# The opening of a fused attention and feed-forward kernel, laid out anew up to its first product with w_out

## The chip, the cores and the metric

The kernel runs on one core of one Trainium2 chip. A core has five engines with a queue of instructions each: TensorE (PE in the profile), VectorE (DVE), ScalarE (ACT), GpSimd (POOL) and SyncE (SP). Each engine works through its own queue in order; between engines semaphores keep the order of data. Loads and stores are issued from SP, ACT and POOL and carried by 16 DMA engines. The metric is the device time of one execution in microseconds; less is better.

## The reference

Two layers follow each other. The first is linear attention with decay over 64-row blocks, for 4 batches, 8 heads, 768 rows and 64 columns a head:

```python
for b in range(nb):
    intra = einsum('bhic,bhjc->bhij', qb, kb) * Dmask[None]
    intra = einsum('bhij,bhjd->bhid', intra, vb)
    inter = einsum('bhid,bhde->bhie', qb * lam_pow[None], kv_state)
    out[:, :, sl] = intra + inter
    kb_dec = kb * rev_pow[None]
    kv_state = lam_block[None, :, None, None] * kv_state + einsum('bhsd,bhse->bhde', kb_dec, vb)
```

`Dmask`, `lam_pow`, `rev_pow` and `lam_block` are powers of a decay `lam`, one per head. The second layer takes the result as 3072 tokens of 512 columns:

```python
h = x @ w_in                                   # 512 x 2048
g = maximum(h, 0) + alpha * minimum(h, 0)      # alpha per column of w_in
return g @ w_out                               # 2048 x 512
```

Inputs and output are 32-bit floats; the products run in 16-bit floats.

## The kernel before, in words

**Tiling.** The attention uses blocks of 128 rows, two at a time (256 rows, even and odd rows apart). Tokens go in six chunks `c` of 512: 256 rows of two batches (`bi` 0 and 1). A *unit* is one chunk, one batch and one half of the heads (`hh`): `units[n]`, so chunk 0 holds units 0 to 3 (units 0 and 1 are batch 0, units 2 and 3 batch 1), chunk 1 units 4 to 7. Of the two blocks of chunk 0 the first has no state before it.

**Steps of a unit.** `load` (L85 to L92, from SP, 32-bit) and `load16` (L102, from POOL, cast to 16 bits on the way) bring keys, queries and values; a whole load covers both halves of the heads, and with a part it covers one. `hold` (L85) writes one element of the tile of a later key load from DVE; that load, in SP's queue, can be issued only after it. `cast` makes 16-bit keys (`"k"`) or queries (`"q"`) on the engine that the call names (A is ACT, V is DVE, G is POOL). `turn` transposes keys and queries on PE into the bank `tp` (tag `tk`), and `turned` copies them to `qkT`. `key_decayed` multiplies keys by their decay (`kdec`), `decayed` does so with the queries (`qdT`). `cluster(old, new)` is the unit pair's work on PE: for `old` its queries times the state before (L389, from `RD`) and the masked scores times values (L409), for `new` its scores (L365) and keys times values (L426). With `True` its result goes into the banks b0 and b1 that the second layer uses as well, otherwise into `acc`. `masked` is DVE's product of scores and decay mask (L438). `state` keeps or updates the state (`KV` on ACT at L473 and L476, `R` on DVE), `spread` writes it into `RD`, and `out_of` copies the attention's result into `xT`.

**The second layer.** `up(c, f, bi, slot)` multiplies 128 columns of w_in by `xT` into bank b0, b1 or b2 (`slot`): 512 wide for `bi` None, 256 wide for one batch (four products each, L511). `below` takes the negative part on ACT (L522), `gate` combines both on DVE with `oma`, which is 1 - alpha (L534); only after that is the bank free. `down` multiplies by w_out (L544), `store` writes out. `load_win(i)` and `load_wout(i)` bring a quarter of the weights each, from POOL. w_in's first quarter serves columns `f` 0 to 3.

**Decays.** lam is loaded from ACT's queue first of all. `logs` takes its logarithm (DVE L198, ACT L199), `logs_by_pair` lays it out by pairs of heads (L203, L204), `mask_logs(hh)` makes four mask logarithms on DVE (L217) and `mask_exp(hh)` their Exp on ACT (L228); `key_decay`, `state_decay` and `query_decay` are Exp on ACT too. `zeros` fills the eight `RD` tiles with zeros on DVE (L177). `positions` and `distances` make the row distances (POOL, then DVE, `pos_f` last at L195). `identity` makes the matrix that transposes need, on POOL. `slopes` turns alpha on PE and makes `oma`.

**Fills.** `fill(n, slot)` issues n matmuls of 128x128 of a constant tile into a bank, whose result nobody reads (L257).

**What sets the order.** The kernel is written with its order by hand: each call in the list emits its instructions at once on the queues of its engines, in the order of the list, and no scheduler moves them. Buffers come from pools with few copies (five raw key tiles, one tile of scores per half pair, one `tp`), so a step also waits until the former user of its buffer is done. The list runs from `light()` into the third chunk; then a woven loop takes over.

## Time and profile before

| What | Value |
|---|---|
| median of 3 runs | 217.8 us (217.76 to 218.54) |
| the profiled execution | 217.74 us |
| its span | 216.0 us |
| PE busy | 208.6 us (97%), 2224 matmuls |
| DVE, ACT, POOL busy | 136.9, 113.3, 88.9 us |
| granted clock of PE, mean | 1.00 |
| fills before the first w_in product | 163 |
| first w_in product starts | 19.69 us |
| first w_out product starts | 42.27 us |

The profile's busy shares are sums over stages of different kinds: PE's first 8.88 us are fills alone. A row of the timeline gives start, length, engine, line, operation, and in brackets the idle time before it with what ended it. Consecutive instructions of an engine overlap by a little, so the start of the next row, not the end of the length, tells how long an instruction keeps its engine. The time of a load runs from its issue until its data is there.

### The profile page before, as it was taken

What the parts mean: (1) busy time and instruction counts of PE and PEld (TensorE: products, weight loads), DVE (VectorE), ACT (ScalarE), POOL (GpSimd) and SP (SyncE); (2) the same over time, 40 slices, a digit from 0 to 9 for tenths busy, and PEclk for the clock granted to TensorE, in tenths of its full rate; (3) what the DMA queues carried; (4) which work ended last, traced back from release to release, by engine and by line L of the source; (5) the groups of instructions that cost most, each with busy time, mean ns of one, the idle gap of its engine ahead of it and who ended that gap; (6) DMA issues with size and microseconds to landing.
All of it is one profiled execution on the core that took longest, in us unless ns stands there. A gap on an engine that the chain in (4) does not pass through costs nothing.

```text
span 216.0 us, 5454 instructions
## 1 busy us (share of the span) xinstructions
PE 208.6 (97%) x2224; PEld 114.7 (53%) x2224; DVE 136.9 (63%) x280; ACT 113.3 (52%) x222; POOL 88.9 (41%) x146
## 2 busy tenths in 40 slices
PE   8979899989999999999999999999999999999994
PEld 8958555544544555546554554554545444444442
DVE  3976999868597878888976646645746344435000
ACT  3777778841657645548745545545435534444120
POOL 8759547760088890193557266256221000000000
PEclk9999999999999999999999999999999999999999
DMA  5999999999999999987999242193011011110212
GB/s 131 218 195 223 203 210 251 214 167 190 314 273 154 253 157 195 180 178 191 196 279 177 40 100 72 25 100 84 16 49 49 5 49 49 49 43 8 97 49 99
DMA packets 63288, 29.85 MB, mean 138 GB/s; under 512 B 34192, under 2 KB 61088, under 8 KB 63264
## 3 DMA queue, kind: packets, MB, share of 16 engines
q1 hardware_dynamic: 38400, 15.01, 35.0%
q0 software_dynamic: 20368, 8.26, 31.9%
q10 hardware_dynamic: 4496, 6.24, 9.1%
q8 instruction: 17, 0.28, 0.6%
q14 instruction: 7, 0.06, 0.1%
HBM read 27.28 MB, written 6.29 MB: 155 GB/s over the span
## 4 chain that ended last, share of the span: by engine, by line
PE 89%; DVE 4%; ACT 3%; DMA 2%; issue 1%; DVEq 0%; ACTq 0%
PE h_ps L511 38%; PE o_ps L544 32%; PE o_ps L569 6%; PE s L365 4%; PE acc L409 3%; PE acc L389 2%; DMA lam_sb<-in_lam_dram 2%; PE acc L426 1%; DVE dmask L217 1%; DVE RD L177 1%; ACT m L522 1%; DVE g L534 1%; PE op_fill L257 1%; PE tp L318 1%; ACT RD L267 1%
## 5 line engine op out<-in xcount | busy, mean ns | idle before, releaser
L534 DVE SCALAR_TENSOR_TENSOR g<-m,oma,h_ps 128x512 f16<-128x512 f32 (+1 forms) x104 | 72.6, 704 | 50.0 <-ACT m L522 49.2
L511 PE MATMUL h_ps<-xT,w_in_sb 128*128 128x512 f16 (+1 forms) x416 | 95.7, 363 | 0.7 <-DVE g L534 0.7
L522 ACT ACTIVATE m<-h_ps 128x512 f32<-128x512 f32 (+1 forms) x104 | 57.9, 564 | 59.3 <-PE h_ps L511 56.9
L544 PE MATMUL o_ps<-w_out_sb,g 128*128 128x512 f16 x320 | 79.4, 379 | 0.7 <-DVE g L534 0.7
L511 PEld LDWEIGHTS <-w_in_sb 128*128 128x128 f16 x416 | 39.4, 98 | 42.3 <-issue 1.6
L544 PEld LDWEIGHTS <-g 128*128 128x128 f16 x320 | 30.5, 98 | 35.8 <-issue 1.0
L271 POOL COPY RD<-R 64x128 f16<-64x128 f16 x46 | 13.4, 290 | 52.0 <-DVE R L481 47.6
L438 DVE TENSOR_TENSOR sm<-s,dmask 128x512 f16<-128x512 f32 x48 | 31.9, 684 | 3.3 <-PE s L365 3.2
L267 ACT ACTIVATE o_sb<-o_ps 128x512 f32<-128x512 f32 (+1 forms) x24 | 14.2, 593 | 23.1 <-PE o_ps L544 12.5
L347 POOL TENSOR_TENSOR qdT<-qkT,qdecay 128x512 f16<-128x512 f16 (+1 forms) x21 | 20.5, 976 | 9.3 <-ACT qkT L267 4.4
L298 POOL TENSOR_TENSOR kdec<-kraw,kdecay 128x512 f16<-128x512 f32 x19 | 19.9, 1049 | 2.1 <-PE acc L426 1.9
L267 ACT ACTIVATE xT<-acc 128x512 f16<-128x512 f32 x19 | 11.3, 597 | 5.9 <-PE acc L426 4.5
L569 PE MATMUL o_ps<-w_out_sb,g 128*128 128x512 f16 (+2 forms) x80 | 14.0, 336 | 0.0
L257 PE MATMUL op_fill<-spark 128*128 128x128 f16 x163 | 12.5, 243 | 1.2 <-DVE one L183 1.1
L481 DVE SCALAR_TENSOR_TENSOR R<-R,rdecay,acc 128x64 f16<-128x64 f16 x48 | 11.2, 275 | 3.6 <-ACT xT L267 1.9
L257 PEld LDWEIGHTS <-spark 128*128 128x128 f16 x163 | 11.3, 111 | 1.7 <-DVE one L183 1.1
L271 POOL CAST qk<-kraw 128x512 f16<-128x512 f32 x14 | 9.0, 645 | 7.5 <-ACT RD L267 6.7
L102 POOL DMA_DIRECT2D vh<-in_v_dram x13 | 11.7, 904 | 0.0
L569 PEld LDWEIGHTS <-g 128*128 128x128 f16 x80 | 7.2, 98 | 6.9
L365 PE MATMUL s<-qkT 64*64 64x128 f16 x384 | 10.4, 222 | 0.0
L409 PE MATMUL acc<-sm,vh 64*64 64x128 f16 x352 | 9.0, 217 | 0.0
L389 PEld LDWEIGHTS <-RD 128*128 128x128 f16 x80 | 6.3, 98 | 4.8 <-ACT RD L267 0.4
(73 smaller groups left out, 126.3 us busy)
## 6 DMA issues: line engine op xcount, KB each, us to landing
kraw<-in_k_dram SPq DMA_DIRECT2D x10, 512.0 KB, 6.8
out_dram<-o_sb ACTq DMA_DIRECT2D x17, 256.0 KB, 3.0
qraw<-in_q_dram SPq DMA_DIRECT2D x8, 512.0 KB, 7.1
vh<-in_v_dram POOLq DMA_DIRECT2D x11, 256.0 KB, 7.4
w_in_sb<-in_moe_w_in_dram POOLq DMA_DIRECT2D x4, 512.0 KB, 9.5
w_out_sb<-in_moe_w_out_dram POOLq DMA_DIRECT2D x4, 512.0 KB, 8.7
out_dram<-o_sb ACTq DMA_DIRECT2D x12, 128.0 KB, 2.0
kraw<-in_k_dram SPq DMA_DIRECT2D x4, 256.0 KB, 5.3
```

Source lines behind the costliest of these rows:

```text
L257: nc.tensor.matmul(t[:, 0:128], lhsT=spark, rhs=spark, start=True, stop=True)
L267: nc.scalar.activation(out, in_, AF.Copy)
L271: nc.gpsimd.tensor_copy(out=out, in_=in_)
L298: engine(eng).tensor_tensor(out=kdec, in0=kr, in1=d.unsqueeze(3).to_broadcast([128, 2, 4, D]), op=ALU.mult)
L347: engine(eng).tensor_tensor(out=qdT[:, :, :, p], in0=t["qkT"][:, 0, :, :, p], in1=qdecay[:, hh, :, :, p], op=ALU.mult,)
L365: nc.tensor.matmul(s[hl][ds(a * 64, 64), hp, 1 - e, :].rearrange("p (e j) -> p e j", e=2), lhsT=t["qkT"][p, 1, e, hp, ds(a * 64, 64)], rhs ...
L438: nc.vector.tensor_tensor(out=t["sm"][hl], in0=t["s"][hl], in1=mask_of(hl, units[n][2]), op=ALU.mult)
L511: nc.tensor.matmul(h_ps[:, 0:n] if bi is None else h_ps[:, 0:n].rearrange("p (e j) -> p e j", e=2), lhsT=w_in_sb[:, gi, ts(f, 128)], rhs=x ...
L522: nc.scalar.activation(m[:, 0:n], HP[c, f, bi][:, 0:n], AF.Relu, scale=-1.0)
L534: nc.vector.scalar_tensor_tensor(out=g, in0=mv, scalar=oma[:, f : f + 1], in1=hv, op0=ALU.mult, op1=ALU.add)
L544: nc.tensor.matmul(O[c, t], lhsT=G[c, f][:, t // 2, t % 2, :], rhs=w_out_sb[:, f, :], start=(f == 0), stop=(f == NF - 1),)
L569: nc.tensor.matmul(o_ps[:, 0:n], lhsT=G[c, f][:, t // 2, t % 2, :], rhs=w_out_sb[:, f, ds(c0, n)], start=(f == 0), stop=(f == NF - 1),)
```

## The change

Only the hand-written list between `distances()` and the first `gate(0, 15, None)` differs; every function is the same, and so is the list behind it. The same steps are called, apart from fills: 163 fills stand ahead of the first `down` before, 160 after. The calls are in another order, and some are on other engines: the key casts of units 0 and 5 go from POOL to ACT, those of units 3, 4 and 6 from ACT to POOL; `key_decayed` of units 1, 4 and 5 from DVE to POOL, of unit 2 from POOL to DVE; `decayed` of units 2 and 5 from POOL to DVE; `turned` of unit 5 from ACT to DVE, of unit 6 from DVE to ACT; `out_of` of unit 2 from DVE to ACT, of units 3 and 4 from ACT to DVE; `spread` of unit 4 from POOL to ACT, of unit 5 from ACT to POOL. Before the first transposes, in brief:

- `zeros()` stands ahead of `logs()`, behind it before;
- the first queries are loaded ahead of the first keys on SP; POOL's first load is the first values, not queries;
- `hold("k", 0, 1, 0)` stands behind `logs_by_pair()`, and `load("k", 0, 1, 1)` ahead of `load("k", 0, 1, 0)`;
- `load_alpha()` stands ahead of `logs()`.

The diff, cut to the part up to the first products with w_in and the last lines:

```diff
     distances()
+    load16("v", 0, 0, 0)
+    zeros()
+    load("q", 0, 0, 0)
+    fill(12, 2)
     load("k", 0, 0, 0)
+    fill(34, 3)
+    fill(14, 1)
+    fill(6, 3)
+    load_alpha()
     logs()
-    load("q", 0, 0, 0)
-    load16("q", 0, 1)
-    hold("k", 0, 1, 0)
-    fill(40, 0)
-    fill(1, 3)
-    load16("q", 0, 0, 1)
-    zeros()
-    fill(6, 3)
-    fill(38, 0)
-    mask_logs(1)
+    fill(5, 1)
+    identity()
+    cast(0, "k", "A")
     cast(0, "q", "A")
     logs_by_pair()
+    state_decay()
+    hold("k", 0, 1, 0)
+    mask_logs(0)
+    mask_logs(1)
+    load16("q", 0, 0, 1)
+    turn(0)
+    query_decay(0, 1)
     key_decay()
-    identity()
-    load_alpha()
-    fill(14, 2)
+    query_decay(2, 1)
+    turned(0, "V")
+    fill(2, 1)
+    mask_exp(1)
     load("k", 0, 0, 1)
+    cast(1, "k", "V")
+    query_decay(1, 1)
+    slopes(2)
+    load16("v", 0, 0, 1)
+    load16("q", 0, 1)
+    load16("v", 0, 1)
+    fill(18, 1)
+    key_decayed(0, "V")
+    load("k", 0, 1, 1)
+    load_win(0)
+    fill(8, 0)
+    load16("q", 1, 0)
+    decayed(0, "G")
+    fill(10, 1)
     load("k", 0, 1, 0)
-    cast(0, "k", "G")
-    mask_exp(1)
-    turn(0)
-    mask_logs(0)
-    fill(3, 1)
-    fill(12, 1)
-    fill(7, 2)
-    load("k", 0, 1, 1)
-    key_decayed(0, "V")
+    cast(2, "k", "A")
+    turn(1)
+    fill(7, 1)
+    mask_exp(0)
+    cluster(None, 0)
+    load16("v", 1, 0)
+    turned(1, "V")
+    key_decayed(1, "G")
+    hold("k", 2, 1)
+    query_decay(3, 1)
+    key_decayed(2, "V")
+    fill(13, 2)
+    fill(11, 3)
+    state(0, 0)
+    turn(2)
+    masked(0, 1)
+    hold("k", 1, 0)
+    decayed(1, "G")
+    cast(3, "k", "G")
+    load_win(1)
+    masked(0, 0)
+    spread(0, 1, "A", True)
+    cluster(0, 1, True)
+    spread(1, 1, "A", True)
+    key_decayed(3, "G")
+    turned(2, "V")
+    turn(3)
+    masked(1, 1)
+    masked(1, 0)
+    turned(3, "V")
+    cluster(1, None)
+    out_of(0, "A")
+    cluster(None, 2)
     hold("k", 3, 0)
-    load16("v", 0, 0, 0)
...
-    out_of(0, "A")
-    decayed(2, "G")
-    spread(1, 1, "A", True)
-    masked(1, 0)
+    decayed(2, "V")
+    masked(2, 1)
+    out_of(1, "A")
+    up(0, 0, 0, 2)
+    decayed(3, "G")
+    masked(2, 0)
+    load_win(2)
     state(1, 0)
-    cluster(1, None)
-    load_win(2)
...
+    load_win(3)
+    up(0, 1, 0, 1)
     spread(2, 1, "A", True)
...
+    up(0, 2, 0, 0)
+    cluster(2, 3, True)
+    below(0, 0, 0)
     below(0, 1, 0)
...
     up(0, 15, None, 2)
     cluster(None, 6)
+    below(0, 14, None)
     out_of(5, "A")
     up(1, 1, 0, 1)
+    up(1, 2, 0, 0)
+    turn(7)
+    gate(0, 14, None)
     below(0, 15, None)
-    up(1, 2, 0, 0)
-    gate(0, 13, None)
-    gate(0, 14, None)
-    turn(7)
+    fill(7, 2)
+    cast(8, "k", "G")
     down(0, 0, 0, 2)
```

## The prediction

> **What bounds the kernel now.** I read the page's busy table first, then busy time by stretches of the span, then TensorE's waits over the rest of the span, then the chain that ended last, in order of time, and then the timeline and the DMA issues of the opening.

> The page: the span, and TensorE's (PE's) share of it.

> ```profile
> span 216.0 us, 5454 instructions
> PE 208.6 (97%) x2224; PEld 114.7 (53%) x2224; DVE 136.9 (63%) x280; ACT 113.3 (52%) x222; POOL 88.9 (41%) x146
> ```

> Busy time by stretch (start:end, length, then us and instructions of PE, PEld, DVE, ACT, POOL, then granted clock, DMA share, GB/s), cut where PE's work changes.

> ```profile
> 0.00:8.88 8.88, 7.77 (x99) 7.63 (x100) 5.52 (x23) 4.82 (x8) 7.88 (x20) 1.00 0.88 159
> ...
> 19.69:42.27 22.58, 21.79 (x331) 13.52 (x322) 20.90 (x43) 18.00 (x41) 15.05 (x24) 1.00 1.32 219
> 46.23:216.00 169.77, 166.56 (x1513) 83.91 (x1502) 100.70 (x194) 80.74 (x148) 57.22 (x93) 1.00 0.63 121
> ```

> PE's waits from 40 us to the end, the only row of the answer:

> ```profile
> PE o_ps L544 <- DVE g L534: 0.7, 1, 0.7
> ```

> From 46.23 us on PE never waits long enough to be listed, and the list of steps there is unchanged. So a lead or a delay that PE has when the products with w_out begin should come out at the end, one for one. The change is worth what it moves PE at that point. The first 8.88 us hold only fills (matmuls whose result nobody reads), so PE's busy share says nothing there. From 19.69 to 42.27 PE and DVE are both nearly full (21.79 and 20.90 of 22.58 us).

> The chain that ended last, its opening part (start, length, what):

> ```profile
> 0.74 3.76 DMA lam_sb<-in_lam_dram
> ...
> 4.74 0.27 DVE RD L177
> ...
> 6.93 1.19 DVE dmask L217 x4
> ...
> 8.60 1.41 DVE dmask L217 x4
> ...
> 12.21 0.38 PE tp L318 x4
> ```

> It is a DVE chain: lam lands at 4.50, eight zero fills stand until 6.93, then the decay logarithms, key work, the first qkT, and only then PE's second transposes at 12.21.

> **The change, part by part.** The durations are in the timeline (start, us, engine, line, operation); for the spacing of two instructions I take the difference of their starts.

> ```profile
> 1.06 7.99 PE L257 MATMUL op_fill<-spark 128*128 128x128 f16 x99 [1.06 <-DVE one L183]
> 2.20 1.84 POOL L102 DMA_DIRECT2D qh<-in_q_dram  x2
> 2.29 0.29 DVE L195 CAST pos_f<-pos_i 128x256 f32<-128x256 int32 x1
> 5.43 2.41 POOL L102 DMA_DIRECT2D vh<-in_v_dram  x3
> 5.68 0.63 ACT L267 ACTIVATE qk<-qraw 128x512 f16<-128x512 f32 x1 [0.74 <-DMA qraw<-in_q_dram]
> 6.33 1.28 ACT L232 ACT_TABLE_LOAD   x1
> 7.62 0.49 ACT L232 ACTIVATE kdecay<-loglam,rev_f 128x8 f32<-128x8 f32 x2
> 9.33 1.61 PE L257 MATMUL op_fill<-spark 128*128 128x128 f16 x22
> 10.04 0.84 ACT L228 ACTIVATE dmask<-dmask 128x768 f32<-128x768 f32 x1 [1.03 <-DVE dmask L217]
> 10.79 1.26 ACT L240 ACTIVATE qdecay<-pos_f,llp 128x128 f32<-128x128 f32 x4
> 13.40 0.69 DVE L438 TENSOR_TENSOR sm<-s,dmask 128x512 f16<-128x512 f32 x1 [1.24 <-PE s L365]
> 16.43 0.66 ACT L267 ACTIVATE xT<-h_acc 128x256 f16<-128x256 f32 x2 [1.00 <-PE h_acc L426]
> 16.98 0.55 ACT L267 ACTIVATE RD<-h_acc 64x128 f16<-64x128 f32 x2
> 17.55 0.45 ACT L476 ACTIVATE KV<-h_acc 128x128 f32<-128x128 f32 x2
> 19.69 1.05 PE L511 MATMUL h_ps<-xT,w_in_sb 128*128 128x256 f16 x8
> 20.45 0.71 ACT L522 ACTIVATE m<-h_ps 128x256 f32<-128x256 f32 x2
> 20.89 0.86 DVE L534 SCALAR_TENSOR_TENSOR g<-m,oma,h_ps 128x256 f16<-128x256 f32 x2
> 24.00 1.02 ACT L267 ACTIVATE qkT<-tp 128x1024 f16<-128x1024 f16 x1
> 25.87 1.89 PE L511 MATMUL h_ps<-xT,w_in_sb 128*128 128x512 f16 x8 [0.52 <-DVE g L534]
> 27.61 2.10 DVE L534 SCALAR_TENSOR_TENSOR g<-m,oma,h_ps 128x512 f16<-128x512 f32 x3 [0.19 <-ACT m L522]
> ```

> The loads of the opening (tile, issuer, KB in the tile, us from issue to landing), in the order of their issue: the first keys, the first queries, keys of the third part, queries, values, w_in, keys of chunk 1.

> ```profile
> kraw<-in_k_dram SPq DMA_DIRECT2D x1, 256.0 KB, 4.1
> qraw<-in_q_dram SPq DMA_DIRECT2D x1, 256.0 KB, 4.4
> kraw<-in_k_dram SPq DMA_DIRECT2D x1, 256.0 KB, 5.9
> qh<-in_q_dram POOLq DMA_DIRECT2D x1, 128.0 KB, 6.5
> vh<-in_v_dram POOLq DMA_DIRECT2D x1, 128.0 KB, 6.8
> w_in_sb<-in_moe_w_in_dram POOLq DMA_DIRECT2D x1, 512.0 KB, 9.4
> kraw<-in_k_dram SPq DMA_DIRECT2D x1, 512.0 KB, 8.2
> ```

> 1. Zero fills ahead of the logarithms. The 8 x 0.27 us now follow pos_f (2.58) and end at 4.76, in DVE's idle time before lam lands at 4.50. They cost 0.25 us there and free 2.19 later. Pair copies follow (0.48, from 8.12 to 8.60), then eight mask logarithms (1.2 to 1.4 for four): done at about 8.3 instead of 10.0.

> 2. First casts. Queries are now issued first on SP and keys second; both have landed at 5.65. The cast of the first keys goes from POOL to ACT, so ACT has two casts of 0.53 to 0.63, and the table load for Exp starts at 6.85 instead of 6.33. ACT is 0.5 us later there. Behind it come four small decays (0.3 each) and one mask Exp (0.75); ACT is through at 10.4.

> 3. The third keys (unit 2's). The one-element write that holds their load back now stands behind the pair copies: SP issues at about 5.7, not 4.7. With the row's 5.9 us they land at 11.6. ACT's cast of them stands ahead of the mask Exp of the first pairs, so ACT waits from 10.4 to 11.6, and that Exp runs 12.15 to 13.0 instead of 10.04 to 10.88. This is the new wait. (Unit 3's keys, which no held-back load stands ahead of on SP any more, are issued at about 2.3 and land before them; nothing waits for those.) Behind it on ACT are one decay, the copy of state 0 and its spread (to 14.1); DVE waits with the first masked product, PE with the first product with a state.

> 4. PE. Fills before the first transposes fall from 99 to 71: 28 fewer at 1.61/22 = 0.073 us, so 9.05 becomes 7.0, when both casts are ready (6.85). The turn of alpha behind them waits for a load that ACT now issues at 2.75; by the SP rows of 4.1 to 5.9 us it lands at 6.9 to 8.7. I take 8.2, near the upper row, because POOL's loads run beside it. Then 36 fills (2.4) reach 10.7. The second transposes need queries which POOL now issues second (about 3.9, after one issue of 0.92 and the identity): with 6.5 us they land at 10.4. So these transposes run at 10.5 to 11.2, before at 12.21. After 7 fills come scores and the state product (to 12.4, values landed long before: issued first, 2.20 + 6.8 = 9.0), and 24 fills (1.6) reach 13.9.

> 5. To the first w_in product. Unit 2's transposes 13.9 to 14.65; masked products (0.69 each, spaced 0.6) 13.0 to 14.4; qkT copy to 15.35; cluster of units 0 and 1 14.65 to 15.5; unit 3's transposes to 16.3; two masked products and the copy to 17.2 on DVE; spread 0.55, xT 0.66 on ACT to 16.75; last product of unit 1 to 16.95; its xT 0.6 to 17.6. w_in's first quarter is issued at 7.2 instead of 7.8 and lands at 7.2 + 9.4 = 16.6. The first product with w_in starts at 17.8; before, at 19.69. The lead is 1.9, partly because the 28 fills that stood here before are gone.

> 6. What takes part of it back. Three products (0.44 each) now stand ahead of cluster 2/3, which writes into the banks of two of them: it waits for ACT's spread (18.0 to 18.55), three negative parts (0.35 spaced) and two gates (0.43): 19.75 instead of 19.1, a new 0.65 us. Then 11 fills (0.7) stand where PE waits for the spread of unit 3 anyway (21.35). Unit 4's keys, held until 13.7 instead of 12.1, land at 13.7 + 8.2 = 21.9; POOL casts them by 22.5, where PE has waited 0.55. ACT's copy of that qkT (1.02) ends at 24.1 and starts unit 4's scores, another 0.25. The first full-width product starts at 25.1. Before it started at 25.87, but the scores and state of unit 4 (0.47) were still to come: the lead is 25.87 + 0.47 - 25.1 = 1.24.

> 7. From there on the same products go through three banks, each with a negative part on ACT (0.6) and a gate on DVE (0.7). Followed queue by queue, PE stands idle at three banks (0.2, 0.35 and 0.25 us), and the two early columns of chunk 1 end at 40.6. The start of unit 7's transposes marks that place:

> ```profile
> 41.82 0.61 PE L318 MATMUL tp<-ident,qk 128*128 128x128 f16 x8
> ...
> 44.03 1.02 PE L544 MATMUL o_ps<-w_out_sb,g 128*128 128x512 f16 x4 [0.74 <-DVE g L534]
> ```

> The 7 new fills ahead of the first product with w_out stand in the 0.74 us that PE waits there for a gate, so they are covered; were that cover gone, they would cost 0.45. The moves of values, w_in and w_out on POOL's queue keep the total bytes before each need and are counted at nothing: the w_out loads come earlier, the second w_in quarter at 14.6 lands by 24 and is needed at 25.1. If it were 1 us later than that, PE would wait.

> **Sum:** 41.8 - 40.6 = 1.2 us off the span. The profiled execution took 217.74 (span 216.0 and 1.74 around it), 0.06 under the median of 217.8. The forecast is 217.8 - 1.2 = 216.6.

> [...]

> **Rivals.** *The lead goes to the gates (less gain).* From 19.69 DVE is 93% busy, and between the first full-width product and the last gate I count 15.8 us for it (17 gates of 0.43 or 0.7, four masked products, four states, three copies or products of 0.3 to 0.7), about as long as PE's. Against it: DVE was as full before. As a check by sums: PE's fills before the columns of chunk 1 fall from 163 to 153, 10 x 0.066 = 0.65 us. If all else that PE waits for is as long as before, the gain is 0.65 and the time 217.1.

> *Slower: unit 2's keys late.* The place is ACT's cast ahead of the mask Exp. Up to a landing at 11.9 the 24 fills cover it; then each us costs one. At 13.1 the gain is gone. Served in order of issue they stand behind four POOL loads and land at about 12.9: gain 0.2, 217.6. At the 8.2 us of the later keys they land at 13.9: 2.0 us late, 218.6. For it speaks that POOL issues five loads before them; against it that 256 KB took 5.9 us beside two such loads.

> *POOL's first loads late.* If zero fills delay POOL's issue until 4.76, the second queries would land at about 12.4 and all behind shift by 1.5 to 1.9, leaving a loss of 0.5: 218.3. Against it: in this trace three POOL issues beside zero fills took 0.8 us each, like others. [...]

> *More gain.* If the first lead of 1.9 stays whole because unit 4's keys land sooner and the banks are free in time: 215.9.

> **How the numbers follow.** Forecast (gain 0.8 to 1.6) 0.42; gates 0.26; unit 2's keys 0.16; POOL 0.06; more gain 0.10. A difference of 0.5%, 1.09 us, is about what a measurement here can tell. Of the forecast's case 0.31 lies beyond it, with more gain's 0.10 and 0.02 of the gates' that is 0.43 faster. Slower by over 0.5% takes a landing near 14.2 or two of these together: 0.14. The rest, 0.43, is the same. The forecast's own range is 216.2 to 217.0; the whole range runs from more gain's 215.8 to 218.4, between the late cases' 218.3 and 218.6, and leaves out under 2 in 10.

> **What would show it.** Right: second transposes near 10.5, an ACT wait of about 1.2 us for unit 2's keys near 10.4, first w_in product near 17.8, full-width product near 25.1, no new PE wait after 46. Wrong: that ACT wait over 2.5 us, PE waiting for queries, or PE waits of over 1.5 us in sum between 25 and 41.

## The result, and the profile after

The changed kernel took 219.14 us in the median of 20 executions (217.28 to 223.9), the kernel before 217.77 (217.53 to 218.54) beside it. The ratio is 1.005, with a 95% interval of 1.0034 to 1.0066: half a per cent slower, where 0.5% faster was forecast. (The ratio leaves out disturbed executions, the medians do not.) Besides its middle, the spread has changed: 6.6 us between lowest and highest, against 1.0.

The profiled execution took 218.54 us. Its page (span; busy us, share and matmuls; the granted clock of TensorE in 40 slices; the queue that brings instructions, with packets, MB and share):

```profile
span 216.6 us, 5445 instructions
...
PE 209.7 (97%) x2221; PEld 115.5 (53%) x2221; DVE 137.1 (63%) x280; ACT 111.8 (52%) x221; POOL 90.3 (42%) x147
...
PEclk9999699999999999999999999999999999999999
...
q8 instruction: 17, 0.28, 0.5%
```

The clock row has a 6 in its fifth slice; before, all 40 slices have a 9. Busy time by stretch, with the same columns as before:

```profile
18.90:21.60 2.70, 0.80 (x30) 0.54 (x32) 2.38 (x5) 1.24 (x5) 0.70 (x2) 1.00 1.35 214
21.60:24.30 2.70, 2.70 (x64) 2.29 (x64) 0.65 (x2) 2.06 (x7) 1.75 (x3) 0.62 1.25 207
24.30:27.00 2.70, 2.70 (x50) 2.10 (x48) 0.65 (x3) 1.69 (x3) 2.41 (x4) 0.75 1.24 207
27.00:42.78 15.78, 15.55 (x183) 8.71 (x181) 14.56 (x29) 11.19 (x23) 8.19 (x12) 1.00 1.31 216
47.05:216.60 169.55, 166.55 (x1511) 83.86 (x1502) 100.76 (x194) 80.75 (x148) 57.55 (x94) 1.00 0.63 122
```

In 18.90 to 21.60 PE works for only 0.80 of 2.70 us; for 5.4 us after that it is busy all the time, at a granted clock of 0.62 and then 0.75. The long run of products with w_out starts at 47.05 (before 46.23), and the rest takes 169.55 (before 169.77). So the whole loss arises ahead of 47, as the prediction's first part said it must; what it missed lies between 19 and 27. PE's timeline there:

```profile
7.02 0.80 PE L318 MATMUL tp<-ident,qk 128*128 128x128 f16 x8
...
10.04 0.39 PE L318 MATMUL tp<-ident,qk 128*128 128x128 f16 x4
...
17.43 1.48 PE L511 MATMUL h_ps<-xT,w_in_sb 128*128 128x256 f16 x12
19.47 0.27 PE L389 MATMUL h_acc<-qdT,RD 128*128 128x128 f16 x2 [0.55 <-DVE g L534]
19.67 0.42 PE L365 MATMUL s<-qkT 64*64 64x128 f16 x16
19.92 0.23 PE L409 MATMUL h_acc<-sm,vh 64*64 64x128 f16 x3
21.50 0.38 PE L409 MATMUL h_acc<-sm,vh 64*64 64x128 f16 x13 [1.35 <-issue]
...
21.93 1.09 PE L257 MATMUL op_fill<-spark 128*128 128x128 f16 x11
...
42.78 0.61 PE L318 MATMUL tp<-ident,qk 128*128 128x128 f16 x8
```

Up to 19.5 PE runs at about the forecast times or ahead of them: first product with w_in at 17.43 (before 19.69), a lead of 2.26 us. Then, after 3 of 16 products of one group, PE stands 1.35 us, and the releaser is "issue": it waited for nothing that the profile shows. The eleven fills behind it take 1.09 us, at a granted clock of 0.66 from 21.93 to 22.93; in the kernel below with unit 4's keys let go later they take 0.79, and twelve of them in the kernel before, at a granted clock of 1.00, take 0.84. At the transposes of unit 7 the lead of 2.26 has become a lag of 0.96 (42.78 against 41.82).

### The profile page after: what moved, and what is told of

It reads as the page before. It is cut to its first block, busy times and chain, and to the rows that moved or that the text cites. A ratio compares the mean times of both kernels' runs of the same rounds, so it can differ in the third digit from the quotient of the medians.

```text
span 216.6 us, 5445 instructions
## 1 busy us (share of the span) xinstructions
PE 209.7 (97%) x2221; PEld 115.5 (53%) x2221; DVE 137.1 (63%) x280; ACT 111.8 (52%) x221; POOL 90.3 (42%) x147
## 4 chain that ended last, share of the span: by engine, by line
PE 94%; DVE 2%; ACT 1%; issue 1%; DVEq 0%
PE h_ps L511 38%; PE o_ps L544 33%; PE o_ps L569 6%; PE op_fill L257 6%; PE s L365 4%; PE acc L409 3%; PE acc L389 2%; PE tp L318 2%; PE acc L426 1%; DVE g L534 1%; DVE sm L438 1%; ACT m L522 1%; PE tp L314 0%; DVE qkT L269 0%; ACT xT L267 0%
## 5 line engine op out<-in xcount | busy, mean ns | idle before, releaser
L534 DVE SCALAR_TENSOR_TENSOR g<-m,oma,h_ps 128x512 f16<-128x512 f32 (+1 forms) x104 | 72.6, 704 | 52.0 <-ACT m L522 51.3
L511 PE MATMUL h_ps<-xT,w_in_sb 128*128 128x512 f16 (+1 forms) x416 | 96.1, 365 | 0.2 <-DVE g L534 0.2
L522 ACT ACTIVATE m<-h_ps 128x512 f32<-128x512 f32 (+1 forms) x104 | 58.2, 564 | 60.3 <-PE h_ps L511 58.5
L544 PE MATMUL o_ps<-w_out_sb,g 128*128 128x512 f16 x320 | 79.4, 379 | 0.1
L511 PEld LDWEIGHTS <-w_in_sb 128*128 128x128 f16 x416 | 39.9, 99 | 42.0 <-issue 1.2
L544 PEld LDWEIGHTS <-g 128*128 128x128 f16 x320 | 30.5, 98 | 35.2 <-issue 0.4
L438 DVE TENSOR_TENSOR sm<-s,dmask 128x512 f16<-128x512 f32 x48 | 31.9, 684 | 0.7 <-PE s L365 0.6
L267 ACT ACTIVATE o_sb<-o_ps 128x512 f32<-128x512 f32 (+1 forms) x24 | 14.2, 593 | 23.1 <-PE o_ps L544 12.5
L298 POOL TENSOR_TENSOR kdec<-kraw,kdecay 128x512 f16<-128x512 f32 x21 | 22.0, 1049 | 2.3 <-PE acc L426 2.0
L347 POOL TENSOR_TENSOR qdT<-qkT,qdecay 128x512 f16<-128x512 f16 (+1 forms) x19 | 19.3, 1015 | 3.4 <-ACT qdecay L240 2.1
L271 POOL CAST qk<-kraw 128x512 f16<-128x512 f32 x15 | 9.4, 633 | 15.8 <-ACT RD L267 6.7
L257 PE MATMUL op_fill<-spark 128*128 128x128 f16 x160 | 12.6, 245 | 1.1 <-DVE one L183 1.1
L481 DVE SCALAR_TENSOR_TENSOR R<-R,rdecay,acc 128x64 f16<-128x64 f16 x48 | 11.2, 275 | 3.7 <-ACT xT L267 1.9
L267 ACT ACTIVATE xT<-acc 128x512 f16<-128x512 f32 x17 | 10.2, 598 | 5.6 <-PE acc L426 4.5
L102 POOL DMA_DIRECT2D vh<-in_v_dram x13 | 11.9, 918 | 0.0
L257 PEld LDWEIGHTS <-spark 128*128 128x128 f16 x160 | 11.2, 112 | 1.3 <-DVE one L183 1.1
L365 PE MATMUL s<-qkT 64*64 64x128 f16 x384 | 10.3, 222 | 0.0
## 6 DMA issues: line engine op xcount, KB each, us to landing
kraw<-in_k_dram SPq DMA_DIRECT2D x10, 512.0 KB, 8.0
out_dram<-o_sb ACTq DMA_DIRECT2D x17, 256.0 KB, 2.9
qraw<-in_q_dram SPq DMA_DIRECT2D x8, 512.0 KB, 8.4
vh<-in_v_dram POOLq DMA_DIRECT2D x11, 256.0 KB, 7.9
w_in_sb<-in_moe_w_in_dram POOLq DMA_DIRECT2D x4, 512.0 KB, 10.0
w_out_sb<-in_moe_w_out_dram POOLq DMA_DIRECT2D x4, 512.0 KB, 11.1
out_dram<-o_sb ACTq DMA_DIRECT2D x12, 128.0 KB, 2.0
kraw<-in_k_dram SPq DMA_DIRECT2D x4, 256.0 KB, 5.1
```

The source lines that it names most:

```text
L257: nc.tensor.matmul(t[:, 0:128], lhsT=spark, rhs=spark, start=True, stop=True)
L267: nc.scalar.activation(out, in_, AF.Copy)
L271: nc.gpsimd.tensor_copy(out=out, in_=in_)
L298: engine(eng).tensor_tensor(out=kdec, in0=kr, in1=d.unsqueeze(3).to_broadcast([128, 2, 4, D]), op=ALU.mult)
L347: engine(eng).tensor_tensor(out=qdT[:, :, :, p], in0=t["qkT"][:, 0, :, :, p], in1=qdecay[:, hh, :, :, p], op=ALU.mult,)
L365: nc.tensor.matmul(s[hl][ds(a * 64, 64), hp, 1 - e, :].rearrange("p (e j) -> p e j", e=2), lhsT=t["qkT"][p, 1, e, hp, ds(a * 64, 64)], rhs ...
```

## The experiments

Three theories stood at the start. **A:** PE's instructions arrive late. PE's list here has 4462 entries (a weight load and a product for each matmul, and some waits); the queue q8 above brings 17 packets of 16 KB (0.28 MB). I took such a packet for 256 entries; the burst below bears that out, where PE stands every 128 products, which are 256 entries. Such a packet is called a piece below; a border is the entry at which a piece begins (192, 448, 704 and so on), and a piece is entered when PE gets to its border. Counted in the list, PE stands exactly ahead of entry 704. **B:** a wait for data or a bank that the profile doesn't name. **C:** the clock alone: it falls because PE has stood for the gates, and the products slow down. In the kernels below line numbers are a few higher than in the changed kernel wherever a helper was added.

### Fills with a quarter of the instructions

```diff
-        for _ in range(n):
+        wide = spark.unsqueeze(1).to_broadcast([128, 4, 128])
+        for _ in range(n // 4):
+            nc.tensor.matmul(t[:, 0:512], lhsT=spark, rhs=wide, start=True, stop=True)
+        for _ in range(n % 4):
             nc.tensor.matmul(t[:, 0:128], lhsT=spark, rhs=spark, start=True, stop=True)
```

> The changed kernel with its fills made as products of 512 columns, one for every four of 128: the same TensorE time, 198 instructions fewer on TensorE's queue (4264 instead of 4462), nothing else changed. In the changed kernel TensorE stands 1.35 us at 19.92 to 21.50, after 3 of 16 products of the scores with the values, for nothing that the profile shows.
> Theory A (instructions come late): TensorE's instructions are loaded in pieces of 256, piece borders at instruction 192, 448, 704 of its list; a piece is asked for when the one before it is entered, and takes 5 to 7 us while data fills the DMA engines (entered at 14.55, the next one usable at 21.45). With 512-column fills instruction 704 is reached near 26 us, 9 us after 448: no stand at the products with the values near 20 us. Instruction 448 now lies in the last state product of unit 1 at 17.3, 5 us after 192: a stand of 0 to 1.9 us may appear there. TensorE's clock stays at 1.00 unless that new stand is long. Time 216.3 to 217.5.
> Theory B (a wait for data or a bank that the profile doesn't name): the stand stays with the instruction, 1.0 to 1.6 us at the same products, time 218.5 to 219.5.
> Theory C (the clock alone): the products slow down whenever TensorE has stood 0.55 us for the gates; the stand may shrink but the granted clock falls to about 0.6 to 0.75 from 21 to 27 us, time 218.5 or more.

Measured: 217.12 us in the median (216.55 to 221.93), ratio to the kernel before 0.9978 (0.9957 to 1.0000). PE's timeline of the profiled execution (217.04 us, span 215.0):

```profile
17.15 0.62 PE L429 MATMUL acc<-vh,kdec 64*64 64x64 f16 x16 [0.47 <-ACT xT L270]
17.70 1.49 PE L514 MATMUL h_ps<-xT,w_in_sb 128*128 128x256 f16 x12
19.73 0.27 PE L392 MATMUL h_acc<-qdT,RD 128*128 128x128 f16 x2 [0.55 <-DVE g L537]
19.94 0.42 PE L368 MATMUL s<-qkT 64*64 64x128 f16 x16
20.18 0.41 PE L412 MATMUL h_acc<-sm,vh 64*64 64x128 f16 x16
...
22.55 0.62 PE L321 MATMUL tp<-ident,qk 128*128 128x128 f16 x8 [0.40 <-POOL qk L274]
...
40.88 0.61 PE L321 MATMUL tp<-ident,qk 128*128 128x128 f16 x8
...
47.23 5.12 PE L547 MATMUL o_ps<-w_out_sb,g 128*128 128x512 f16 x23 [0.18 <-DMA w_out_sb<-in_moe_w_out_dram]
```

The 16 products with the values at 20.18 now run without a break. A smaller loss has come where theory A put it, in the state product that holds entry 448 (0.62 us at 17.15 for what takes 0.32). The data, the banks and the 0.55 us for the gate are the same, so B and C fall as causes of the stand. The clock can still fall without it: in 3 of the 12 executions its mean was 0.992, and these took 219.44 to 221.93 us. PE reaches unit 7's transposes at 40.88: 1.90 sooner than the changed kernel, 0.94 ahead of the kernel before.

The same edit in the kernel before:

> The kernel before with the same 512-column fills (216 instructions fewer on TensorE's queue). Theory A: the 0.23 us that TensorE stands in the scores of unit 3 at 20.78 to 21.02 (instruction 704 in this kernel too) are gone; 448 is reached 6 us after 192, so 0 to 0.9 us may appear near 19.5; time 217.2 to 218.3. Theories B and C: no change but noise, 217.6 to 218.0, and the 0.23 us stay.

It gave 217.53 us, ratio 0.9988 (0.9978 to 0.9998). Here theory A's expectation failed: the scores at 20.53 still take 0.66 us instead of 0.42, though entry 704 now lies elsewhere. That these 0.23 us of the kernel before lie beside entry 704 is chance. In both kernels one of the 16 products runs, and the second starts 0.05 us after DVE's masked product (L438, here L441) has ended: 21.02 after 20.97 before, 20.78 after 20.72 here. So they are most likely a wait for that product, which reads the tile that the scores write.

### More instructions in the fills

```diff
-        for _ in range(n):
-            nc.tensor.matmul(t[:, 0:128], lhsT=spark, rhs=spark, start=True, stop=True)
+        for _ in range(2 * n):
+            nc.tensor.matmul(t[:, 0:64], lhsT=spark, rhs=spark[:, 0:64], start=True, stop=True)
```

> The changed kernel with every fill of 128 columns made of two of 64 columns: 320 instructions more on TensorE's queue, the same columns. Theory A: instruction 704 comes forward to the scores of units 0 and 1 at 14.2 us, 4.3 us after 448: a stand of 0.8 to 2.6 us there, and a second one of up to 1.4 us at instruction 960, in the scores of units 2 and 3 near 19.8; the stand in the products with the values goes; time 218.5 to 221. Theory B: the stand stays at the products with the values, 1.35 us, and none comes at 14.2; time as the changed kernel's. Theory C: as B.

Measured: 221.67 us, above the 218.5 to 221 expected, ratio 1.0184 (1.0164 to 1.0205). PE's timeline:

```profile
16.86 0.38 PE L365 MATMUL s<-qkT 64*64 64x128 f16 x13 [0.66 <-issue]
...
29.36 0.22 PE L426 MATMUL acc<-vh,kdec 64*64 64x64 f16 x2 [1.72 <-issue]
```

The stand left the products with the values and went to the scores of units 0 and 1, again after 3 of 16 (entry 704). The second came not at entry 960 but at 1216. PE gets to 960 at 23.3, 6.4 us after 704, and doesn't stand there. Adding instructions that do the same work slows the kernel further; not all of it is the two stands, since the opening is late before the first (second transposes at 10.81, 10.04 in the changed kernel) and PE waits 0.81 us there for decayed queries from POOL.

### Fewer and more transfers in flight

```diff
     masked(0, 1)
-    hold("k", 1, 0)
...
     cluster(2, 3, True)
     below(0, 0, 0)
+    hold("k", 1, 0)
```

> The changed kernel with the one-element write that holds back the 512 KB load of unit 4's keys moved behind the first gate (from 12.9 to about 19.5 us): TensorE's list is unchanged, only fewer transfers run from 13 to 20 us. Theory A: the piece of instructions that came at 19.0 comes at 16.5 to 17.5, and the stand of 1.35 us in the products with the values is gone or under 0.3 us; cluster 2/3 with its state product is through at about 20.6 instead of 21.9. Unit 4's keys then come at 25 to 28, and TensorE waits 2 to 4 us for its transposes: 219 to 222. Theories B and C: the stand of 1.0 to 1.6 us stays where it was, and the wait for unit 4's keys adds to it: 220 to 223.

Measured: 226.36 us, in a single execution. The stand shrinks from 1.35 to 0.43 us after the same three products (PE goes on at 20.49), and the packet comes at 18.27 instead of 19.05: A's direction, but not its size (16.5 to 17.5, under 0.3 us). PE then waits 8.37 us for unit 4's keys, not 2 to 4.

```diff
     hold("k", 1, 0)
+    hold("k", 1, 1)
...
     load("k", 1, 0)
+    load("k", 1, 1)
...
-    hold("k", 1, 1)
...
-    load("k", 1, 1)
```

> The changed kernel with one more load in flight from 13 to 20 us: unit 5's and the following unit's keys (512 KB) are let go together with unit 4's, instead of at about 25 us. TensorE's list is unchanged.
> Theory A1 (the loads hold the piece of instructions up): its packet comes after 19.0, at 20 to 22, and the stand at the products with the values grows from 1.35 to 2 to 4 us; time 219.5 to 222.
> Theory A2 (a piece takes about 6 us whatever moves): the stand stays at 1.0 to 1.6 us; 218 to 219.5, apart from what w_in's or unit 4's keys lose by it.

Measured: 218.63 us, ratio 1.0035 (1.0016 to 1.0054). The stand is 1.35 us again and the packet at 19.28, so this reading of A missed. It was no test of it, though: the added load is issued at 13.51, but between entry and packet (14.6 to 19.27 us) the queues moved 0.95 MB, in the changed kernel (14.45 to 19.05) 0.93, at 203 and 201 GB/s. No more traffic ran in that time.

### A burst where the DMA engines are quiet

```diff
+    burst(128)          # 512 products of 64x64 by 64x128, as in scores
     for t in range(4):
         down_last(NC - 1, t, [DM] if t < 3 else [384, 128])
```

> The changed kernel with 512 products of 64x64 by 64x128 whose result nobody reads (the form of the scores, 16 of them in 0.25 us, 1024 instructions on TensorE's queue: 8 us if nothing holds them up) put ahead of the last four products with w_out, where the DMA engines carry only a store now and then (25 to 97 GB/s, DMA share 0.1 to 0.2). Borders of the pieces lie after 124, 252, 380 and 508 of the 512 products.
> Theory A1 (a piece takes 5.7 to 6.9 us in the opening because it shares the DMA engines with the loads): here each piece takes clearly less, 2 to 4 us; TensorE stands 0 to 2 us at each border, the burst lasts 8 to 16 us, time 227 to 235.
> Theory A2 (a piece takes about 6 us whatever else moves): TensorE stands 3.5 to 4.5 us at each of the four borders, the burst lasts 22 to 26 us, time 240 to 245.
> Theory B (no border of instructions): no stand, or one elsewhere; 227.

Measured: 230.74 us, in a single execution. PE's timeline:

```profile
199.57 3.71 PE L1173 MATMUL burst<-spark 64*64 64x128 f16 x252
204.64 1.98 PE L1173 MATMUL burst<-spark 64*64 64x128 f16 x128 [1.36 <-issue]
208.10 1.98 PE L1173 MATMUL burst<-spark 64*64 64x128 f16 x128 [1.47 <-issue]
211.55 0.25 PE L1173 MATMUL burst<-spark 64*64 64x128 f16 x4 [1.47 <-issue]
```

The DMA queues of the same kernel from 199.6 to 211.7 us (packets, MB, share of 16 engines):

```profile
q10 hardware_dynamic: 288, 0.26, 6.4%
q8 instruction: 3, 0.05, 1.6%
```

PE stands after 252, 380 and 508 products, as counted; only the first border of the four passes unseen. Pieces of 128 products run in 1.98 us and come every 3.46. So even with hardly any other traffic (6.4% of the 16 engines) a piece took 3.46 us from the moment the one before it was entered; in the opening it took this long:

| Kernel | border | entered (us) | packet (us) | PE goes on (us) | entered to use | packet to use |
|---|---|---|---|---|---|---|
| burst | 5056 | 204.64 | 205.75 | 208.10 | 3.46 | 2.35 |
| changed | 704 | 14.45 | 19.05 | 21.50 | 7.05 | 2.45 |
| narrow fills | 704 | 10.7 | 14.61 | 16.86 | 6.2 | 2.25 |
| narrow fills | 1216 | 23.3 | 27.02 | 29.36 | 6.1 | 2.34 |
| later keys of unit 4 | 704 | 14.4 | 18.27 | 20.49 | 6.1 | 2.22 |
| before, zero fills first (below) | 704 | 14.6 | 18.62 | 21.00 | 6.4 | 2.38 |

"Entered" is read from the timeline at entry 256 before the border, the packet's start by narrowing the window. From packet to use it is 2.2 to 2.5 us in all six rows. From entry to packet it is 1.1 us in the burst and 3.7 to 4.6 between loads at 188 to 212 GB/s: this is the part that grew beside the opening's loads. In the kernel before, entry 448 is entered at 15.9 and the packet comes at 18.11, 2.2 us later, between loads at 251 GB/s; by the same 2.4 us the piece is there at 20.5, just ahead of entry 704 at 20.78. By this estimate the old layout was 0.3 us from the stand, and nothing in its profile told so.

That a piece is asked for when the one before it is entered is my reading of these rows: in each of the six the packet comes after that entry, by 1.1 to 4.6 us. No run shows the request itself.

### The stand without the slow clock

```diff
     up(0, 2, 0, 0)
+    wide_fill(2, 3)     # two products of 512 columns
     cluster(2, 3, True)
```

> The changed kernel with two products of 512 columns (0.5 us, 4 instructions) put where TensorE stands 0.55 us for a gate, right before cluster 2/3; instruction 704 is then after 1 of the 16 products with the values.
> Theory A, with the clock as a result of standing (0.55 and 1.35 us close together, then 0.62 and 0.75 of the clock from 21.6 to 27 us): the stand for instructions stays, 1.0 to 1.6 us at the same place; with the gate's wait filled, the clock is 1.00 in most runs and the time comes to 217.5 to 218.3.
> Theory C (the standing for instructions is enough for the clock to fall): the clock falls as before, time 218.5 to 219.5.

Measured: 218.7 us, ratio 1.0021 (0.999 to 1.0051). PE's timeline:

```profile
20.28 0.22 PE L416 MATMUL h_acc<-sm,vh 64*64 64x128 f16 x1
21.86 0.41 PE L416 MATMUL h_acc<-sm,vh 64*64 64x128 f16 x15 [1.36 <-issue]
```

The stand is as long, and again exactly ahead of entry 704, now after one product. The clock stayed at 0.998 or more in 8 of 10 executions, and in 8 of 20 of the changed kernel. So one stand of 1.36 us mostly left the clock alone; 0.55 and 1.35 us within 2.6 us mostly did not. That the sum of standing decides isn't shown: with all fills wide (0.30 and 0.55 us) 3 of 12 executions lost the clock, in the aligned kernel below (0.38 and 0.78 us) 1 of 12. From cluster 2/3 to unit 7's transposes it is 22.34 us here, 23.31 in the changed kernel and 21.15 with wide fills: the stand costs about 1.2 net of the wait for keys that it hides, the slow clock about 1.0. The time was still above the forecast: with the clock at full, executions lie between 217.28 and 220.24. What spreads them isn't settled.

### Single parts of the change

```diff
     load("k", 0, 0, 0)
+    zeros()
     logs()
...
-    zeros()
```

> The kernel before with one part of the change alone: the eight zero fills ahead of the decay logarithms on VectorE.
> If the zero fills are what the opening's lead comes from: the second transposes come from 12.21 to about 11.0 (the end of the fills ahead of them), the first product with w_in from 19.69 to about 18.5, and the time to 216.6 to 217.2.
> If the opening's lead needs the other moves too (fewer fills, the loads' order, the casts): second transposes move, but the later fills, ScalarE's decays or the loads take it back: first product with w_in within 0.4 of 19.69, 217.4 to 217.9.

Measured: 217.79 us, ratio 0.9983 (0.9967 to 0.9998), an unchanged median. PE's timeline of the kernel before with its zero fills moved, and DVE's row for the gates in question:

```profile
10.86 0.38 PE L318 MATMUL tp<-ident,qk 128*128 128x128 f16 x4 [0.65 <-DVE kraw L85]
...
18.41 1.05 PE L511 MATMUL h_ps<-xT,w_in_sb 128*128 128x256 f16 x8
...
21.00 0.42 PE L365 MATMUL s<-qkT 64*64 64x128 f16 x16 [1.43 <-DVE g L534]
```

```profile
19.60 0.86 DVE L534 SCALAR_TENSOR_TENSOR g<-m,oma,h_ps 128x256 f16<-128x256 f32 x2
```

The same scores in the kernel before as it was:

```profile
20.78 0.65 PE L365 MATMUL s<-qkT 64*64 64x128 f16 x16
```

Neither expectation holds whole. The zero fills alone bring the first product with w_in 1.28 us forward, and PE then stands 1.43 us ahead of the scores of unit 3: the lead is gone by 21. The profile puts this wait down to a gate, but that can't be it. Both gates had ended by 20.47, 0.53 us before PE goes on, where PE goes on within 0.06 us of the other gates that it waits for; and in the kernel before the same scores begin at 20.78, while the same two gates run from 20.89 to 21.75. What fits is entry 704. The trace counts 350 products of PE ahead of this stand, as it does ahead of the one in the changed kernel, and the packet comes at 18.62, 2.38 us before PE goes on. So the zero fills alone, with PE's list as it was, bring the kernel before to the border 1.3 us sooner and into the same stand. The estimate of 0.3 us above is borne out, and the new order of PE's list isn't needed for the stand.

The other way round, in the kernel with all fills wide:

```diff
-    zeros()
     load("q", 0, 0, 0)
...
     logs()
+    zeros()
     fill(5, 1)
```

> The changed kernel with the 512-column fills, and one part undone: the zero fills stand behind the decay logarithms again.
> If the prediction's first step is right (2.19 us freed on the chain lam, logarithms, key work, second transposes): second transposes at 11.5 to 12.3 instead of 10.17, first product with w_in 1.5 to 2.2 us later than 17.70, time 218.3 to 219.3 against 217.1.
> If the zero fills don't matter (another chain sets the opening): 217.0 to 217.5.

Measured: 224.76 us in the median of five executions (219.52 to 225.2); the ratio of 1.007 (1.0038 to 1.0101) rests on two of them, 219.52 and 219.65. Second transposes come at 11.82 instead of 10.17, as the first step has it. The profiled execution (224.76) lost its clock as well (a mean of 0.985), after PE had waited 2.04 us for a cast of keys and 0.99 for a product on POOL, and its first product with w_in comes 5.7 us later, not 1.5 to 2.2. That is more than I expected: the new order leans on these 2 us.

### Can the borders be laid better?

```diff
-    fill(14, 1)
-    fill(6, 3)
+    narrow_fill(14, 1)  # 128 columns, as in the changed kernel
+    narrow_fill(6, 3)
...
     up(0, 2, 0, 0)
+    fill(8, 3)
     cluster(2, 3, True)
```

> The changed kernel with 512-column fills, except that 20 fills before the first transposes stay at 128 columns, so that instruction 192 comes 24 instructions sooner and 448 lies at the end of the scores of unit 2, where TensorE waits for ScalarE's xT anyway; and two products of 512 columns fill the 0.55 us for the gate before cluster 2/3.
> Theory A: the 0.3 us in the last state product of unit 1 (17.15 to 17.77 for what takes 0.31) are gone or covered, first product with w_in at 17.3 to 17.5 instead of 17.70, clock 1.00 in nearly all runs, time 216.3 to 217.0.
> Theories B and C: as the run with 512-column fills alone, 217.0 to 217.3, with some runs at 219 and more.

Measured: 217.42 us, ratio 0.9971 (0.9955 to 0.9988). Entry 448 does lie at the end of the scores, but PE stands there until 17.33, and the first product with w_in comes at 17.67, no sooner than with all fills wide: the opening ran 0.27 us later here (second transposes at 10.44, not 10.17), so the piece of entry 448 came hardly sooner (packet at 14.88, with all fills wide 15.05). The gate's wait grew to 0.78 us behind the two fills that were to cover it. The time is above the 216.3 to 217.0 expected, and what the alignment is worth stays open.

```diff
-    fill(12, 2)         # all fills up to about 9 us back to 128 columns
+    narrow_fill(12, 2)
...
-    fill(18, 1)
+    narrow_fill(18, 1)
     fill(8, 0)          # these and the later ones: 512 columns
```

> The changed kernel with some of its fills as 512-column products, chosen so that the borders spread over the opening: instruction 192 entered near 9.0 us, 448 needed near 14.9, 704 near 20.9, gaps of about 6.0 us, where a piece took 5.7 to 6.9.
> Theory A: stands of 0 to 0.9 us at the end of the state product of units 0 and 1 (448) and at the 11 fills behind cluster 2/3 (704), the latter before a wait that PE has anyway; clock 1.00 in nearly all runs; time 216.6 to 217.4, with fewer runs over 219 than with all fills wide.
> Theory B: the stand of 1.35 us stays at the products with the values; 218.5 to 219.5.

The stand is 0.47 us at entry 704, as counted, and yet the time is 218.21, above the 216.6 to 217.4 expected, ratio 1.0028 (1.0001 to 1.0056). PE's timeline:

```profile
21.09 0.38 PE L264 MATMUL op_fill<-spark 128*128 128x512 f16 x1 [0.47 <-issue]
...
23.87 0.62 PE L327 MATMUL tp<-ident,qk 128*128 128x128 f16 x8 [1.78 <-POOL qk L280]
```

PE waits 1.78 us for unit 4's keys, whose cast runs on landing, at 23.2 here, 21.88 with all fills wide. That raised a new question: what limits the lead once the stand is gone?

### The loads behind the stand

In the kernel with wide fills the chain of work between 16 and 23 us is one load: `13.35 8.48 DMA kraw<-in_k_dram`, unit 4's keys. So they were let go sooner:

```diff
     hold("k", 2, 1)
+    hold("k", 1, 0)
...
-    hold("k", 1, 0)
```

> The changed kernel with 512-column fills, and the one-element write that holds back unit 4's keys moved ahead of the first masked product: it comes at 11.6 instead of 13.26 us, so SP issues that load 1.6 us sooner. With 512-column fills alone these keys were cast at 21.88, on landing, and TensorE waited 0.40 us for them; in other kernels of this study they were cast as late as 23.2 and 23.6.
> If that landing is what TensorE's lead hangs on: they are cast at 20.3 to 21.0, the wait of 0.40 us is gone, the transposes of unit 4 start at 22.1 to 22.2, and the time is 216.3 to 216.9, with fewer runs above 217.5.
> If the loads only share the DMA engines differently: they land at 21 to 22 all the same, or the piece of instructions at 448 comes later (a stand over 0.6 us near 17.3): 217.0 to 217.6.

Measured: 217.32 us, ratio 0.9985 (0.9962 to 1.0007). PE's timeline:

```profile
21.96 0.62 PE L321 MATMUL tp<-ident,qk 128*128 128x128 f16 x8
...
40.29 0.61 PE L321 MATMUL tp<-ident,qk 128*128 128x128 f16 x8
...
47.22 5.12 PE L547 MATMUL o_ps<-w_out_sb,g 128*128 128x512 f16 x23 [0.59 <-DMA w_out_sb<-in_moe_w_out_dram]
```

The wait for the keys is gone and unit 7's transposes come at 40.29, a lead of 1.53 us. But PE goes on at 47.22, to 0.01 us where it did without this: the third load of w_out lands then. So the loads of chunk 2 were moved behind it:

```diff
     load_wout(1)
-    hold("k", 2, 0)
...
     gate(0, 4, None)
+    hold("k", 2, 0)
...
-    cast(8, "k", "G")
...
-    cast(8, "q", "A")
...
+    cast(8, "k", "G")
+    cast(8, "q", "A")
     turn_by_dma(8)
```

> As the kernel with 512-column fills and unit 4's keys sooner, but the loads of chunk 2's first keys and queries are let go about 4 us later (the one-element write goes from 28.4 to about 32.5 us), and their casts on POOL and ScalarE stand behind the state products of units 6 and 7, so that nobody waits for them sooner.
> If the bytes moved before it set the landing of w_out's third load (the DMA engines are full from 2 to 50 us, some 210 GB/s): it lands 1 to 2.5 us sooner, TensorE's wait of 0.59 us for it is gone, the long run of products with w_out goes on at 46.5 to 46.7 instead of 47.22, and the time is 216.2 to 216.8.
> If its landing is set by its own queue (POOL's), it stays at 47.2 and the wait at 0.4 to 0.8 us; time 217.0 to 217.4.

Measured: 217.33 us, ratio 1.0002 (0.9974 to 1.003). The wait for w_out is gone, and the long run starts without a break at 44.48, 1.75 us ahead of the kernel before. The end is hardly earlier: in the list of PE's waits (line waited for, us in total, times, longest) two new ones stand; the first is for the transposed keys and queries of chunk 2, which are now late.

```profile
PE s L368 <- DMA qkT<-qk: 0.3, 1, 0.3
...
PE acc L392 <- DVE xT L272: 0.2, 1, 0.2
```

| Kernel | lead at unit 7's transposes | span | first wait behind it |
|---|---|---|---|
| wide fills | 0.94 | 215.0 | w_out, 0.18 |
| and unit 4's keys sooner | 1.53 | 215.0 | w_out, 0.59 |
| and chunk 2's loads later | 1.61 | 214.9 | unit 8, 0.3 and 0.2 |

The lead of 0.94 comes out at the end as 1.0; what is won beyond it is lost to the next load. In the kernel with unit 4's keys sooner the DMA share is 1.19 to 1.46 in each stretch of 4 us from 24 to 52, at 206 to 218 GB/s up to 48, and each reordering moved the wait on to whichever load now came last. That their total sets the limit fits all three but wasn't tried by taking bytes away.

Of the thirteen kernels the fastest against the kernel before are the one with all fills wide (0.9978, 0.9957 to 1.0000) and the aligned one (0.9971, 0.9955 to 0.9988), both ahead of the changed kernel too. Their intervals overlap, with each other and with that of the zero fills alone (0.9983). Over all 12 executions their means are 217.89 and 218.05 us, against 218.01 and 217.90 for the kernel before beside them: what they gain in most executions, a few long ones (219.4 to 222.6 us) take back.

## Why the prediction was wrong

**The stage that decides** (first part): right. From 47.05 on nothing is lost, and the delay ahead of it comes out at the end.

**Step 1, zero fills:** right. In the changed kernel they end at 4.83 (4.76 forecast) and the mask logarithms at 8.51 (8.3):

```profile
3.74 1.09 DVE L177 MEMSET RD<- 128x256 uint32 x4
...
5.78 2.73 DVE L217 SCALAR_TENSOR_TENSOR dmask<-rel_f,loglam,future 128x192 f32<-128x192 f32 x8
```

**Steps 2 and 3, casts and unit 2's keys:** half right, in ACT's timeline of the changed kernel:

```profile
6.21 0.63 ACT L267 ACTIVATE qk<-kraw 128x512 f16<-128x512 f32 x1 [1.12 <-DMA kraw<-in_k_dram]
...
10.78 0.61 ACT L267 ACTIVATE qk<-kraw 128x512 f16<-128x512 f32 x1
11.30 0.83 ACT L228 ACTIVATE dmask<-dmask 128x768 f32<-128x768 f32 x1
```

The first keys, issued second, landed 0.55 later than I took; the forecast wait of 1.2 us for unit 2's keys did not come (they had landed by 10.78, 11.6 was forecast), and the mask Exp ran at 11.30 instead of 12.15. Neither rival on late loads came true.

**Steps 4 and 5, PE to the first product with w_in:** right. The 71 fills end at 7.0 as forecast, second transposes at 10.04 (10.5), first product with w_in at 17.43 (17.8).

**Step 6, what takes part back:** this is the step that failed. Each of its terms was right to 0.15 us, and the sum was wrong. Cluster 2/3 waits 0.55 us until 19.47 (0.65 until 19.75). With the stand taken away, PE waits 0.40 us for unit 4's keys (0.55), 0.24 for the qkT copy (0.25), the first full-width product starts at 25.31 (25.1), and unit 7's transposes come at 40.88 (40.6). In the changed kernel the last two are 27.14 and 42.78. The term that fails is one that the sum does not have: it followed PE from wait to wait and gave the work between them its durations, as if PE's own instructions were always there. PE does not work through the 256 entries faster than before (448 to 704: 15.9 to 20.8 before, 14.45 to 20.15 now); the piece comes later. The DMA queues between entry and packet, first of the kernel before (15.9 to 18.2 us), then of the changed one (14.5 to 19.1 us):

```profile
q1 hardware_dynamic: 836, 0.43, 77.2%
q0 software_dynamic: 482, 0.13, 54.7%
```

```profile
q0 software_dynamic: 1831, 0.58, 112.6%
q1 hardware_dynamic: 671, 0.34, 36.0%
```

Before, the entry falls where POOL's loads (q0) have 55%; in the changed kernel it falls 1.5 us sooner, where they have 113%. That this share sets the delay isn't shown: with the zero fills moved alone it was 74% and the packet took 4.0 us from entry, with unit 4's keys let go later 165% and 3.9. What the runs do show is that with the entry 1.3 us sooner (zero fills alone) the packet came 0.5 us later, and with the entry 1.5 us sooner (changed kernel) 0.9 later. From cluster 2/3 to unit 7's transposes the changed kernel takes 23.31 us and the one with wide fills 21.15; the stand (about 1.2 net) and the slow clock (about 1.0) make up the difference, and with it the 2.2 us by which 42.78 is later than the forecast 40.6.

**Step 7, the fills and the loads:** the seven fills ahead of the first product with w_out were covered, as said. Counting the moved loads at nothing was wrong in a way that the changed kernel hides: its lag lets them land in time. As soon as PE is 0.9 us ahead, the third load of w_out is what it waits for, so the forecast of 216.6 lies near the best that was seen of this order without the long stand: with wide fills the median is 217.12, the lowest 216.55.

**The rivals:** the first, that the lead goes to the gates, did not come true: PE waits 0.55 us at a gate there (0.65 forecast), and the 1.43 us that the profile puts down to a gate with the zero fills alone are the stand at entry 704. The slower rivals both named loads of data; the mechanism that decided was in neither, and 219.14 lies outside the range. Of the signs that I listed as proof of error none appeared, since the stand came before 25 us and the slow clock counts as busy time.

## What to carry to other kernels

Count the instructions of a tuned stretch, not only its time: where PE works through 256 of them (128 small matmuls with their weight loads) in less than the 6.1 to 7.05 us that the next piece took in five cases here (about 4.6 in the kernel before, by the estimate above), it may stand, as it did for 0.43 to 1.72 us, and the row says only "issue" or names an engine that had been done for 0.53 us. So compare the end of the instruction named with the start of the one that waited. Fewer and larger instructions for the same time, here fills of 512 columns, are the first remedy: they took the stand from 1.35 us (at entry 704) to 0.30 (at 448). And when a lead is won in a stretch whose DMA engines are full (a share of 1.19 to 1.46 here), ask what the next load to land is: here three in a row took back what was won beyond 0.94 us.
